# Reordering the first loads and the first matmuls of a gated attention and FFN kernel

## The chip, the cores and the metric

The kernel runs on one core of one Trainium2 chip. The metric is the device time of one execution in microseconds (us). A profile lasts from the first to the last instruction, its span, which is about 1.25 us shorter than the time of the same execution.

## The reference, cut to what matters

```python
x = A_x                                             # 1 x 2048 x 640, bf16
g = sigmoid((x * gate_w).sum(-1, keepdims=True))    # the gate row
a = A_ref(x, A_wqkv, A_w_phi, A_wo)                 # linear attention, 32 heads of 20
b = B_ref(x, B_w_gate, B_w_up, B_w_down)            # (silu(x @ w_gate) * (x @ w_up)) @ w_down
return g * a + (1 - g) * b
```

Three inputs matter here: the rows of x (16 tiles of 128 tokens), the value third of wqkv (five row blocks of 128 x 640, called wv0 to wv4 below), and gate_w (640 numbers, which the kernel transposes and appends to wv as one more column, so that the value product yields the gate's sum as well).

## The kernel before

The program is a list of short codes. `LOADS` gives the order of the transfers, `ORDER` that of the work. H is a pair of dummy matmuls, X a tile's five transposes, G the transpose of the gate row, and U t.c the two products of token tile t with row block c of wv.

```python
NWARM = 2
NPEW = 16
LOADS = """
x0 w0 x1 w1 x2 w2 x3 w3 w4 f0 h k0 k1 t4 ...
"""
ORDER = """
H0 H1 H2 H3 H4 H5 H6 H7 H8 H9 X0 G H10 H11 H12 U0.0 X1 H13 U1.0 U0.1 X2 U1.1 U2.0 U0.2 U1.2 U2.1
X3 U2.2 U0.3 U1.3 U2.3 U0.4 U1.4 U2.4 V3 Y F0.1 M1 ...
"""
# ... (cut)
    XQ = ["sp", "act", "act", "act"]             # queue of x0 to x3
    WQ = ["sp", "sp", "sp", "sp", "act"]         # queue of wv0 to wv4
    dma("act", gwr[0:5, :], bass.AP(gate_w.tensor, gate_w.offset, [[P, 5], [1, P]]))
# ... (cut)
    def xpose(t):                                # X
        pr = next_pair()
        for c0, c1 in (((0, 1), (1, 5)) if t < 3 else ((0, 5),)):
            o = bankbf(2 * pr + (c0 > 0), 640)
            transposes([(o[:, c * P:(c + 1) * P], xs[:, t, c * P:(c + 1) * P]) for c in range(c0, c1)])
            copy("dve", xT[:, t, c0:c1, :].rearrange("p c k -> p (c k)"), o[:, c0 * P:c1 * P])

    def gcol():                                  # G
        pr = next_pair()
        o = bankbf(2 * pr, 8)[:, 0:5]
        transposes([(o, gwr[0:5, :])], 5)
        copy("dve", wvg[:, :, D:D + 1], o.unsqueeze(2))
# ... (cut)
    def kv_end():
        for _ in range(NPEW):
            pe.wait_ge(tr.sem["pe"], 1)          # satisfied long before
        kv_finish()
# ... (cut)
```

The dummy matmuls multiply a constant by itself, and nothing reads what they give.

The softmax here doesn't subtract the row's maximum and nothing guards it: scores larger than these inputs give would overflow.

## Time and profile before

| | before |
|---|---|
| time, three runs | 289.95, 290.13, 290.69 us |
| span of the profiled run | 287.6 us |
| TensorE busy | 284.9 us, 99% |
| TensorE's share of the chain that ended last | 99% |
| first product of the gate projection (`xT,wg`) | 11.49 us after the start |

The lines themselves and their reading stand in the prediction.

```profile
11.49 1.24 PE L296 MATMUL ps<-xT,wg 128*128 128x512 bf16 x5
```

Everything ahead of this line is the start-up that the change touches, and what follows it lasts 287.6 - 11.49 = 276.1 us.

### The profile page before, as it was taken

The numbers are of one execution on the slowest core, as the hardware profiler recorded it, in microseconds if no ns is written. First come the engines' busy times: TensorE is split into PE (matmuls) and PEld (weight loads), VectorE is DVE, ScalarE is ACT, GpSimd is POOL, SyncE is SP. The second block draws the span as 40 slices with busy tenths as digits, with TensorE's granted clock in tenths as the row PEclk, the third lists the DMA queues.
The fourth block names the chain that finished last, engine by engine and source line by source line (L and its number), as shares of the span: only waits on it lengthen the run. The fifth ranks groups of instructions, "written<-read, shape, count | busy, mean of one in ns | idle before, by whom it ended". The sixth has DMA issues, their size and how long they took to land.

```text
span 287.6 us, 4959 instructions
## 1 busy us (share of the span) xinstructions
PE 284.9 (99%) x1977; PEld 175.2 (61%) x1977; DVE 163.4 (57%) x243; ACT 151.8 (53%) x252; POOL 159.8 (56%) x125
## 2 busy tenths in 40 slices
PE   8999999999999999999999999999999999999997
PEld 7667777675644545557775556675554446656776
DVE  2237748576469978689991465970317899100000
ACT  0767778676775565683535653225576552234112
POOL 8286999879446789836543438350753558501000
PEclk9999999999999999999999999999999999999999
DMA  7979488000010598202393002061020006210101
GB/s 219 190 133 123 100 251 317 5 1 2 2 47 0 114 297 162 51 2 50 65 158 70 5 1 50 2 149 42 2 50 0 3 1 123 52 46 0 49 23 48
DMA packets 48944, 21.62 MB, mean 75 GB/s; under 512 B 39384, under 2 KB 48792, under 8 KB 48920
## 3 DMA queue, kind: packets, MB, share of 16 engines
q1 hardware_dynamic: 47534, 20.59, 32.0%
q10 hardware_dynamic: 1386, 0.71, 0.9%
q8 instruction: 16, 0.26, 0.4%
q14 instruction: 8, 0.07, 0.1%
HBM read 9.29 MB, written 2.62 MB: 41 GB/s over the span
## 4 chain that ended last, share of the span: by engine, by line
PE 99%; DVE 0%; issue 0%
PE ps L296 97%; PE ps L477 1%; PE ps L308 1%; DVE osb L732 0%
## 5 line engine op out<-in xcount | busy, mean ns | idle before, releaser
L324 POOL TENSOR_TENSOR hT<-hT,us 128x512 bf16<-128x512 bf16 (+1 forms) x56 | 65.0, 1173 | 65.3 <-DVE hT L328 47.0
L328 DVE SCALAR_TENSOR_TENSOR hT<-hT,ps 128x512 bf16<-128x512 bf16 (+1 forms) x56 | 37.4, 683 | 66.9 <-ACT hT L314 53.3
L296 PE MATMUL ps<-xT,wg 128*128 128x512 bf16 x260 | 64.6, 379 | 0.0
L296 PE MATMUL ps<-xT,wu 128*128 128x512 bf16 x260 | 64.6, 379 | 0.0
L296 PE MATMUL ps<-wd,hT 128*128 128x320 bf16 (+2 forms) x462 | 63.9, 295 | 0.0
L324 POOL TENSOR_TENSOR ph<-eq,qc 128x1320 bf16<-128x1320 bf16 x16 | 42.3, 2644 | 25.6 <-DVE qc L637 22.2
L296 PEld LDWEIGHTS ps<-wd,hT 128*128 128x128 bf16 x462 | 44.5, 98 | 17.4
L296 PE MATMUL ps<-wqk,xT 128*128 128x320 bf16 x320 | 47.7, 299 | 0.0
L314 ACT ACTIVATE hT<-ps 128x512 bf16<-128x512 f32 (+2 forms) x60 | 35.8, 596 | 16.7 <-PE ps L296 16.5
L296 PEld LDWEIGHTS ps<-xT,wu 128*128 128x128 bf16 x260 | 25.5, 98 | 30.6
L314 ACT ACTIVATE us<-ps 128x512 bf16<-128x512 f32 (+1 forms) x56 | 33.5, 598 | 19.2 <-PE ps L296 18.2
L314 ACT ACTIVATE osb<-ps,omg 128x640 bf16<-128x640 f32 (+2 forms) x17 | 12.9, 757 | 55.8 <-PE ps L296 55.8
L296 PEld LDWEIGHTS ps<-xT,wg 128*128 128x128 bf16 x260 | 25.1, 98 | 27.8 <-ACT oT L314 0.8
L324 POOL TENSOR_TENSOR ekr<-ekr,krec 128x1280 bf16<-128x1280 bf16 x16 | 37.4, 2357 | 5.8 <-DVE krec L338 5.8
L296 PEld LDWEIGHTS ps<-wqk,xT 128*128 128x128 bf16 x320 | 30.5, 98 | 13.1 <-issue 0.4
L314 ACT ACTIVATE eq<-ps 128x640 bf16<-128x640 f32 x32 | 22.3, 703 | 20.9 <-POOL ph L324 10.7
L335 DVE TENSOR_REDUCE ksum<-ekr 128x64 f32<-128x1280 bf16 x16 | 23.5, 1470 | 11.7 <-ACT ekr L314 11.7
L314 ACT ACTIVATE ekr<-ps 128x640 bf16<-128x640 f32 x32 | 22.3, 703 | 8.7 <-PE ps L296 8.2
L335 DVE TENSOR_REDUCE qz<-eq 128x64 f32<-128x1280 bf16 x16 | 23.7, 1478 | 2.6 <-ACT eq L314 2.6
L296 PE MATMUL ps<-wog,oT 128*128 128x320 bf16 (+2 forms) x165 | 24.7, 294 | 0.0
L296 PE MATMUL ps<-wvg,xT 128*128 128x320 bf16 (+1 forms) x160 | 24.6, 301 | 0.0
L335 DVE TENSOR_REDUCE qw<-ez 128x64 f32<-128x1280 bf16 x16 | 23.6, 1476 | 0.0
(73 smaller groups left out, 190.4 us busy)
## 6 DMA issues: line engine op xcount, KB each, us to landing
out_dram<-osb SPq DMA_DIRECT2D x15, 160.0 KB, 1.9
wd<-in_B_w_down_dram SPq DMA_DIRECT2D x1, 2080.0 KB, 10.7
wg<-in_B_w_gate_dram SPq DMA_DIRECT2D x1, 1040.0 KB, 10.1
wu<-in_B_w_up_dram SPq DMA_DIRECT2D x1, 1040.0 KB, 12.2
wg<-in_B_w_gate_dram SPq DMA_DIRECT2D x1, 800.0 KB, 6.2
wu<-in_B_w_up_dram SPq DMA_DIRECT2D x1, 800.0 KB, 7.8
wog<-in_A_wo_dram SPq DMA_DIRECT2D x2, 375.0 KB, 7.2
wvg<-in_A_wqkv_dram SPq DMA_DIRECT2D x4, 160.0 KB, 4.2
```

Source lines behind the costliest of these rows:

```text
L296: last = pe.matmul(o, lhsT=l, rhs=r, start=st, stop=sp_, skip_group_check=sk)
L308: last = pe.transpose(o, i, ident[0:k, 0:k])
L314: return run("act", lambda: act.activation(o, i, func, scale=scale), rd, [o])
L324: return run(e, lambda: eo.tensor_tensor(o, a, b, op), [a, b], [o])
L328: return run("dve", lambda: dve.scalar_tensor_tensor(out=o, in0=a, scalar=s, in1=b, op0=op0, op1=op1), rd, [o])
L335: return run("dve", lambda: dve.tensor_reduce(o, i, AX.X, ALU.add), [i], [o])
L477: last = pe.matmul(bank(2 * pr, 0, P), lhsT=c, rhs=c, start=True, stop=True)
```

## The change

The intent, as the diff reads: issue wv0 at once on the queue that nobody else uses yet, fill the wait for x0 with dummies, and bring x1's transposes up so that no dummy stands between the first real products.

```diff
-NPEW = 16
+NPEW = 24
 LOADS = """
-x0 w0 x1 w1 x2 w2 x3 w3 w4 f0 h ...
+x0 w0 x1 g w1 x2 w2 x3 w3 w4 f0 h ...
 ORDER = """
-H0 H1 H2 H3 H4 H5 H6 H7 H8 H9 X0 G H10 H11 H12 U0.0 X1 H13 U1.0 U0.1 X2 ...
+H0 H1 H2 H3 H4 H5 H6 H7 H8 H9 H10 H11 H12 X0 G X1 U0.0 U1.0 U0.1 X2 ...
-    WQ = ["sp", "sp", "sp", "sp", "act"]
+    WQ = ["act", "sp", "sp", "sp", "act"]
-    dma("act", gwr[0:5, :], bass.AP(gate_w.tensor, gate_w.offset, [[P, 5], [1, P]]))
+    def load_gate():
+        dma("sp", gwr[0:5, :], bass.AP(gate_w.tensor, gate_w.offset, [[P, 5], [1, P]]))
```

SyncE's queue now holds x0, gate, wv1, wv2, wv3; ScalarE's holds wv0, x1, x2, x3, wv4. There are 26 dummies instead of 28, all of them in front.

More of the change, by code (lines that the diff above doesn't have):

```diff
@@ L33 @@
 LOADS = """
-x0 w0 x1 w1 x2 w2 x3 w3 w4 f0 h k0 k1 t4 k2 k3 k4 t5 t6 t7 t8 t9 t10 t11 t12 t13 t14 t15 q0 q1 q2 q3
+x0 w0 x1 g w1 x2 w2 x3 w3 w4 f0 h k0 k1 t4 k2 k3 k4 t5 t6 t7 t8 t9 t10 t11 t12 t13 t14 t15 q0 q1 q2 q3
 q4 f1 f2
@@ L38 @@
 ORDER = """
-H0 H1 H2 H3 H4 H5 H6 H7 H8 H9 X0 G H10 H11 H12 U0.0 X1 H13 U1.0 U0.1 X2 U1.1 U2.0 U0.2 U1.2 U2.1
+H0 H1 H2 H3 H4 H5 H6 H7 H8 H9 H10 H11 H12 X0 G X1 U0.0 U1.0 U0.1 X2 U1.1 U2.0 U0.2 U1.2 U2.1
 X3 U2.2 U0.3 U1.3 U2.3 U0.4 U1.4 U2.4 V3 Y F0.1 M1 i3 M0 F0.0 M2 V4 M3 M4 K0 K1 I S0 V6 V5 S1 P0
@@ L752, in _build @@
         "M": lambda m: premult(1, m), "R": lambda m: premult(0, m),
-        "K": ktile, "S": knorm, "P": kmul, "p": lambda t: kmul(t, "dve"), "E": kvtile, "x": load_x, "t": load_xt, "w": load_wv, "h": load_phi, "k": lambda m: load_wt(1, m), "q": lambda m: load_wt(0, m),
+        "K": ktile, "S": knorm, "P": kmul, "p": lambda t: kmul(t, "dve"), "E": kvtile, "x": load_x, "t": load_xt, "w": load_wv, "g": load_gate, "h": load_phi, "k": lambda m: load_wt(1, m), "q": lambda m: load_wt(0, m),
         "f": lambda i: load_ffn(FCUT[i], FCUT[i + 1]), "L": load_late_weights, "T": tail_weights, "J": gates,
```

## The prediction

> **What bounds the kernel now.** I read the page first, then the chain of work that ended last, then the first ten microseconds of the timeline engine by engine, then the DMA view cut to one issue at a time. The page's busy line and the chain:
>
> ```profile
> PE 284.9 (99%) x1977; PEld 175.2 (61%) x1977; DVE 163.4 (57%) x243; ACT 151.8 (53%) x252; POOL 159.8 (56%) x125
> ```
> ```profile
> by line: PE ps L296 97.3%; PE ps L477 1.1%; PE ps L308 0.7%; DVE osb L732 0.1%; issue 0.0%
> ...
> 0.84 2.29 PE ps L477 x20
> 3.14 0.82 PE ps L308 x6
> 3.96 0.75 PE ps L477 x6
> 4.71 0.53 PE ps L296 x2
> 5.24 0.52 PE ps L308 x5
> 5.76 0.11 PE ps L477 x2
> 5.87 0.55 PE ps L296 x4
> ```
>
> TensorE is busy for 99% of the span and the chain never leaves it: L296 are the real matmuls, L308 the transposes, L477 the dummy matmuls that only keep the array busy. No transfer and no other engine is a link. So the program takes as long as its matmul stream, and a change pays only where that stream is not at full rate. The timeline of TensorE shows where that is:
>
> ```profile
> 0.84 2.29 PE L477 MATMUL ps<-const-bfloat16-1.0 128*128 128x128 bf16 x20 [0.84 <-PEq L791]
> 3.13 0.71 PE L308 MATMUL ps<-ident,xs 128*128 128x128 bf16 x5
> 3.77 0.18 PE L308 MATMUL ps<-ident,gwr 5*128 5x5 bf16 x1
> 3.89 0.82 PE L477 MATMUL ps<-const-bfloat16-1.0 128*128 128x128 bf16 x6
> 4.50 0.74 PE L296 MATMUL ps<-wvg,xT 128*128 128x320 bf16 x2
> 5.04 0.72 PE L308 MATMUL ps<-ident,xs 128*128 128x128 bf16 x5
> 5.57 0.30 PE L477 MATMUL ps<-const-bfloat16-1.0 128*128 128x128 bf16 x2
> 5.71 0.71 PE L296 MATMUL ps<-wvg,xT 128*128 128x320 bf16 x4
> 6.26 0.44 PE L308 MATMUL ps<-ident,xs 128*128 128x128 bf16 x5
> ```
>
> Read starts against starts, since the ends are modelled and overlap. Two 128x320 matmuls take 5.04 - 4.50 = 0.54 us, so 0.27 each; four take 6.26 - 5.71 = 0.55, so 0.137 each. Five transposes take 0.53 us at 5.04 and 0.28 at 6.26 (the next start in the trace is 6.54). So the array runs at half speed until about 5.65 us and at full speed from there. From then on successive 128x320 matmuls start 0.135 to 0.141 us apart and 128x512 ones 0.216; the only wider starts in the whole remainder are at the sixty-four-column output items (0.23 to 0.31 us). There is nothing left to gain but in the first 5.7 us, and the whole stake there is small.
>
> [...] 0.27 us then 0.137 us for the same matmul, the change 4.8 us after the first dummy at 0.84. The clock row of the page reads 9 throughout and does not show it. [...] the windows of 0.4 us from 2.2 us on carry 330, 198, 285, 352, 320 and 359 GB/s, whichever of the two queues feeds them. [...]
>
> **The change part by part.**
>
> Dummies: 28 before (20, 6, 2), 26 after, all ahead of the first transposes. Before, the 20 start 0.107 us apart from 0.84. Six more give 20 + 6: first start 0.845, then 0.06 and 24 times 0.107, so the last ends at about 3.57 us instead of 2.93. Before, the array then stood until x0 came: it was issued at 0.80 and landed 2.3 us later, 3.1, and the first transpose is at 3.13. So the six dummies fill a hole of 0.2 us before x0 and push the transposes back to about 3.6. After them the six and the two that stood in the way (4.50 - 3.89 = 0.61 us and 5.71 - 5.57 = 0.14 us) are gone.
>
> Loads: the order before was x0, wv0, wv1, wv2, wv3 on SyncE and gate, x1, x2, x3, wv4 on ScalarE. After: x0, gate, wv1, wv2, wv3 and wv0, x1, x2, x3, wv4. wv0 is issued at 0.82 instead of 1.27 and runs beside x0. Two loads of 160 KB are 328 KB; from about 1.9 us at 320 GB/s that takes 1.0 us, and before, x0's last packet was about 0.5 us ahead of its landing. So x0 should land at 3.4 to 3.6 rather than 3.1, wv0 at 3.4 to 3.6 rather than 3.9. That is just when the 26 dummies end, which is plainly why they were moved. x1 before landed at 1.41 + 2.9 = 4.3. After, it shares with wv1, and three tiles plus part of a fourth must have moved by then, as before: I put it at 4.3 to 4.9, 4.6 in the middle. Later rows come in pairs some 1.2 us apart (x2 landed at 1.80 + 3.9 = 5.7, x3 at 2.27 + 4.8 = 7.1, used at 6.26 and 7.91); these keep slack.
>
> TensorE's order: x0's five transposes (0.53 us at half speed) run 3.6 to 4.15, the gate's one to about 4.25, x1's five start at once if x1 is there, 4.25 to 4.8. Then the first product, which needs VectorE's copies of x0 and of the gate column. Before, that last copy ended at 4.22 + 0.17 = 4.39, which is 0.86 after the last transpose started at 3.53. After, the last transpose starts at about 4.03, so the copy ends at 4.9 and the product runs 4.95 to 5.5, and the second tile's product crosses the speed change and ends at about 5.9. Before, that second product ran 5.71 to 5.98. Gain with everything in time: about 0.1 us. With x1 at 4.6: its transposes run 4.65 to 5.2, the first product to 5.7, the second to 5.97. Gain: 0. With x1 at 4.9: a loss of 0.2 to 0.25 us.
>
> NPEW, 16 waits to 24, each already satisfied when it is met: the waits stand near 75.2 to 76.5 us, where TensorE's sequencer is about 1.5 to 2 us ahead of the array. In that stretch the 20 products of 128x320 start 0.136 apart and the next transposes at 77.58, without a hole. Two waits share one sequencer instruction there, about 0.1 us apart, so eight more take about 0.4 us of a lead of at least 1.0 us. Cost: 0.
>
> Sum: -0.25 to +0.25 us on 290.13, with a centre near -0.1.
>
> **The rivals.** (1) The early load of wv0 delays x0 and x1 on the shared engines and the array waits where the dummies were; x1's transposes now stand ahead of the first product, so a late x1 holds everything behind it. For it: the transfers are at 285 to 359 GB/s there. Against: the total ahead of x1 is the same. It would make 290.3 to 290.6. (2) Fewer holes bring the clock's release earlier[...]: dense dummies from 0.84 to 3.57 instead of stops at 3.1 and 3.7. Against: the stops are only 0.2 and 0.14 us. If it came 1 us earlier, half of the cold microsecond is won, 0.5 us: 289.6. (3) The extra waits starve the array near 76 us: at most 0.4 us, 290.5. (4) All of it is hidden[...]: 290.1 as before, within the runs' own spread of 289.95 to 290.69.
>
> **Range and chances.** The centre is 290.13 - 0.1 = 290.0. The parts differ by at most 0.5 us either way, and the runs of before span 0.7, so 289.4 to 290.7 should hold it 8 times in 10. Two per cent is 5.8 us, more than the entire stretch that the change touches, so same gets nearly all.
>
> **What would show it.** In the new profile: the last dummy at 3.47 and x0's transposes near 3.6; x0's load taking 2.6 to 2.8 us to land instead of 2.3; x1's transposes before 4.7 (gain) or after it (rival 1); the second product's starts at 0.137 spacing from about 5.7 (an earlier change of speed is rival 2); the start of the four later products (6.54 before for the next ones) shifted by under 0.3 us; and no wider starts around 76 to 78 us. The prediction is wrong if a tile that is not here counted lands after TensorE needs it, or if the shift in loads moves a later stage by over a microsecond.

In the trace of before, the two queues' shares of the six stretches of 0.4 us are 329 and 0, 195 and 3, 185 and 99, 70 and 281, 182 and 137, 160 and 198 GB/s (SyncE's first).

## The result, and the profile after

| | before | after |
|---|---|---|
| median time | 289.66 us (6 runs, 289.00 to 290.69) | 288.71 us (6 runs, 288.52 to 289.27) |
| ratio | | 0.9968, interval 0.9946 to 0.9991 |
| span of the profiled run | 287.6 us | 287.3 us |
| first gate product | 11.49 us | 11.14 us |
| from there to the end | 276.1 us | 276.1 us |

A ratio here is the mean time of one kernel's fast runs over that of the other's of the same rounds, so it is not quite the ratio of the medians. In this row the kernel before has six times: the three on record and three new ones (289.38, 289.00, 289.15). All three new ones are below all three old ones, which will matter below.

The busy line of the page after the change, and the chain with its pieces:

```profile
PE 284.5 (99%) x1975; PEld 174.7 (61%) x1975; DVE 163.4 (57%) x243; ACT 151.9 (53%) x252; POOL 159.9 (56%) x125
```
```profile
0.84 2.93 PE ps L478 x26
3.77 1.32 PE ps L308 x11
5.09 0.98 PE ps L296 x6
```

The bound is the same, and the chain is still TensorE from end to end. Its pieces show the new order: 26 dummies in a row, then eleven transposes (x0, gate, x1), then products. The timeline of TensorE after:

```profile
0.84 2.93 PE L478 MATMUL ps<-const-bfloat16-1.0 128*128 128x128 bf16 x26 [0.84 <-PEq L792]
3.76 0.72 PE L308 MATMUL ps<-ident,xs 128*128 128x128 bf16 x5
4.41 0.18 PE L308 MATMUL ps<-ident,gwr 5*128 5x5 bf16 x1
4.53 0.57 PE L308 MATMUL ps<-ident,xs 128*128 128x128 bf16 x5
5.08 0.99 PE L296 MATMUL ps<-wvg,xT 128*128 128x320 bf16 x6
5.92 0.44 PE L308 MATMUL ps<-ident,xs 128*128 128x128 bf16 x5
6.20 1.53 PE L296 MATMUL ps<-wvg,xT 128*128 128x320 bf16 x10
...
11.14 1.24 PE L296 MATMUL ps<-xT,wg 128*128 128x512 bf16 x5
```

Six products take 5.92 - 5.08 = 0.84 us, 0.14 each, so the very first product already runs at full speed. Single transposes change from 0.107 to 0.057 us apart at 4.8 us. I call that moment **the release** of the clock. Before, it came between 5.5 and 5.65 us. x3's transposes start at 7.57 instead of 7.91, and the lead of 0.34 us is carried unchanged to the end.

So this profile shows 0.3 us, while the two medians differ by 0.95. The added waits took nothing: the 20 products around them start at 74.87 and hand over at 77.58 before, and at 74.53 and 77.25 after, 2.71 and 2.72 us. The sequencer's records of the waits stand about 0.11 us apart, up to 75.83 before and 75.91 after. The next wait is recorded at 76.48 and 76.14, 1.10 and 1.11 us ahead of the transpose that follows it.

### The profile page after: what moved, and what is told of

Its sections match the earlier page's. It is cut to its first block, busy times and chain, and to the rows that moved or that the text cites. A ratio compares the mean times of both kernels' runs of the same rounds, so it can differ in the third digit from the quotient of the medians.

```text
span 287.3 us, 4960 instructions
## 1 busy us (share of the span) xinstructions
PE 284.5 (99%) x1975; PEld 174.7 (61%) x1975; DVE 163.4 (57%) x243; ACT 151.9 (53%) x252; POOL 159.9 (56%) x125
## 4 chain that ended last, share of the span: by engine, by line
PE 99%; DVE 0%; issue 0%
PE ps L296 97%; PE ps L478 1%; PE ps L308 1%; DVE osb L733 0%
## 6 DMA issues: line engine op xcount, KB each, us to landing
wu<-in_B_w_up_dram SPq DMA_DIRECT2D x1, 1040.0 KB, 12.8
```

## The experiments

Two theories stood at first. **Clock**: the release falls at another moment in each execution, and the change lets it fall earlier. **Schedule**: the gain is the fixed shift of work that the two profiles show, and the rest is noise. A third, that the **waits** gain something, needed one run. Later a **landing** theory joined them: rows that arrive late hold TensorE in some executions. "Hole" below is the distance between two starts less what the first matmul needs at its speed.

### First call: repeat, and take the change apart

**b_again** is the kernel before, unedited.

> The kernel before, unchanged, for its spread and a second profile. Clock theory: TensorE's change from half to full speed falls at a different moment from execution to execution, the spans spread by more than 1 us, the second profile shows the change later than the first one's 5.65 us, and each us that it comes later lengthens the span by about 0.5 us. Schedule theory: the change comes at 5.65 us again (within 0.2 us), and spans agree within 0.3 us.

Measured: 289.64 us median, 289.02 to 291.51; ratio 1.001 (0.9978 to 1.0041). TensorE's timeline of this second profile of before:

```profile
3.83 0.82 PE L477 MATMUL ps<-const-bfloat16-1.0 128*128 128x128 bf16 x6
4.92 0.70 PE L296 MATMUL ps<-wvg,xT 128*128 128x320 bf16 x2 [0.28 <-DMA wvg<-in_A_wqkv_dram]
5.41 0.74 PE L308 MATMUL ps<-ident,xs 128*128 128x128 bf16 x5
5.94 0.42 PE L477 MATMUL ps<-const-bfloat16-1.0 128*128 128x128 bf16 x2
6.16 1.05 PE L296 MATMUL ps<-wvg,xT 128*128 128x320 bf16 x4
```

Two things differ from the first profile of the same kernel. The four products from 6.16 take 7.04 - 6.16 = 0.88 us instead of 0.55, and single starts change from half to full distance between 6.4 and 6.9: the release came a microsecond later. And TensorE stood before the first product. The six dummies take 0.61 us and end at 4.44, but wv0, issued 1.25 us after the start, landed 3.5 us later at 4.8, where the first profile had it at 3.9. The hole is 0.48 us. The first gate product is at 12.27, and 288.4 - 12.27 is again 276.1. So between these two profiles all of the difference lies in the first 12 us, in two terms that the program does not fix: the moment of the release, and rows that land late.

**loads_only** has the new loads alone.

```diff
-ORDER: H0 ... H12 X0 G X1 U0.0 U1.0 U0.1 X2 ...            NPEW = 24
+ORDER: H0 ... H9 X0 G H10 H11 H12 U0.0 X1 H13 U1.0 ...     NPEW = 16     (against after)
```

> The kernel before with only the new load order; TensorE's order and the 16 waits are those of before. Clock theory: x0's transposes start about 3.75 us instead of 3.13, so the hole after the 20 dummies grows to about 0.8 us; if the clock's release depends on how densely the array was kept busy, it comes late, and the time is 0.3 to 1 us over before. Schedule theory: 0.3 to 0.6 us over before, from x0's later landing alone, with the speed change at 5.65 us.

Measured: 290.74 us median, ratio 1.0034 (1.0009 to 1.0059). Its timeline:

```profile
0.84 2.29 PE L478 MATMUL ps<-const-bfloat16-1.0 128*128 128x128 bf16 x20 [0.84 <-PEq L792]
3.77 0.71 PE L308 MATMUL ps<-ident,xs 128*128 128x128 bf16 x5 [0.63 <-DMA xs<-in_A_x_dram]
...
8.03 2.28 PE L296 MATMUL ps<-wvg,xT 128*128 128x320 bf16 x10
```

x0, with wv0 now issued beside it, lands at 3.72 (in the traces of before and after, which differ alike, ScalarE's queue moved 3 and 166 GB/s from 2.6 to 3.0 us, SyncE's 195 and 192), its transposes start at 3.77, and the 20 dummies are over at 2.93: a hole of 0.84 us. Ten products from 8.03 still take 10.14 - 8.03 = 2.11 us instead of 1.37, so the release came only after 9 us. The loads alone lose 0.8 us in the mean of the timed runs.

**order_only** has the new order alone.

```diff
-ORDER: H0 ... H9 X0 G H10 H11 H12 U0.0 X1 H13 U1.0 ...
+ORDER: H0 ... H12 X0 G X1 U0.0 U1.0 ...                    (against before)
```

> The kernel before with only the new order of TensorE's work (26 dummies first, x1 transposed before the first product); loads and the 16 waits are those of before. Clock theory: the array has no hole until 3.6 us, the release comes near 4.9 us or at least earlier than in before on average, and the time is 0.5 to 1 us under before. Schedule theory: 0.15 to 0.35 us under before, as x0 and x1 are there when they are wanted.

Measured: 289.15 us median, 288.68 to 290.80, ratio 0.9993 (0.9963 to 1.0024). In the mean of the timed runs it is 0.25 us under before, which the schedule theory asked for and the clock theory did not, but the interval of the ratio reaches past 1. In its profile x1 landed at 4.86 and TensorE stood 0.55 us ahead of x1's transposes; the release came at 6.2 us.

**a_npew16** is the changed kernel with 16 waits.

```diff
-NPEW = 24
+NPEW = 16
```

> The changed kernel with the 16 waits of before instead of 24. Clock and schedule theories: the same time as the changed kernel (within 0.2 us; 0.9968 of before). Waits theory (the added waits are what gained): back to the time of before.

Measured: 289.09 us median, ratio 0.9987 (0.9961 to 1.0013). Its interval overlaps that of the result, so by time alone the waits are not settled. Its profile settles it: the first gate product is at 12.95 and the span 289.1, again 276.1 us from there to the end. With 16 or 24 waits the rest of the program is equally long, so the waits theory falls. The late start had another cause:

```profile
6.23 0.71 PE L296 MATMUL ps<-wvg,xT 128*128 128x320 bf16 x4
8.54 1.00 PE L296 MATMUL ps<-wvg,xT 128*128 128x320 bf16 x6 [1.59 <-DMA wvg<-in_A_wqkv_dram]
```

wv2 landed at 8.5 us, and TensorE stood 1.76 us. The changed kernel isn't immune to late rows either.

### Second call: more samples, and the clock on purpose

**a2** and **b2** are the two kernels, unedited.

> The changed kernel, unchanged, for more samples beside the kernel before on one chip. So far every span is the start of the first gate product plus 276.11 us, so all of the spread lies ahead of it. If the first measurement (0.9968) was typical, this repeats 0.995 to 0.998; if a good part of it was luck in where the clock's release fell, it is nearer to the 0.9987 of the version with 16 waits. The second profile shows the speed change somewhere between 3.6 and 7.0 us, and span minus first gate product is again 276.1 us.

> The kernel before, unchanged, a third profile: ratio 1.000 within 0.002; the speed change lies somewhere between 5.6 and 9.6 us; if the late first wv rows of the second profile (4.79 us, a hole of 0.48 us in TensorE) are common, they are seen again.

Measured: a2 288.82 us median (288.68 to 289.23), ratio 0.9987 (0.9973 to 1.0). b2 289.37 (288.46 to 290.16), ratio 0.9996 (0.9979 to 1.0013). a2's profile has its release at 6.0 to 6.5 us and its first gate product at 11.72, so the early release of the first profile after was not a property of the kernel, and the ratio repeats a_npew16's 0.9987 rather than the first 0.9968. b2's profile has the release at 6.5 and a late wv2:

```profile
6.94 0.71 PE L296 MATMUL ps<-wvg,xT 128*128 128x320 bf16 x4
8.38 1.00 PE L296 MATMUL ps<-wvg,xT 128*128 128x320 bf16 x6 [0.73 <-DMA wvg<-in_A_wqkv_dram]
```

That is a hole of 0.90 us (8.38 - 6.94 - 0.55), in the same place as in a_npew16.

**two_dummies** is the changed kernel with one dummy pair.

```diff
-H0 H1 H2 H3 H4 H5 H6 H7 H8 H9 H10 H11 H12 X0 G X1 ...
+H0 X0 G X1 ...
```

> The changed kernel with 2 dummy matmuls instead of 26. Clock theory: [...] the busy time now starts at 3.76 us instead of 0.84, so the speed change comes at 6.4 to 9.8 us, some 2.8 us later, and the time is about 1 to 1.4 us over the changed kernel. Schedule theory: x0 lands at 3.7 us whatever stands before it, so no change (within 0.2 us).

Measured: 289.91 us median, ratio 1.0024 (1.0006 to 1.0041), 1.1 us over a2 by medians. The schedule theory's 0.2 falls. Its timeline:

```profile
3.81 0.71 PE L308 MATMUL ps<-ident,xs 128*128 128x128 bf16 x5 [2.60 <-DMA xs<-in_A_x_dram]
...
5.13 1.79 PE L296 MATMUL ps<-wvg,xT 128*128 128x320 bf16 x6
```

The real work stands about where it stood. Six products take 6.71 - 5.13 = 1.58 us, with the release at 7.0. In the first profile after they took 0.84, but in a2's, of the same call, 6.49 - 4.96 = 1.53, with the release at 6.4: one profile against one shows only 0.37 us of span (288.2 against 287.8). In the mean of the timed runs the dummies are worth 1.2 us. That it comes through the clock is what was expected, and the later release agrees, but the single profile doesn't show the whole of it.

**late_start** is the changed kernel with real work held until the clock and the rows are settled.

```diff
# (shortened)
-H0 ... H12 X0 G X1 ...
+H0 ... H32 X0 G X1 ...
-    memset("pool", ident[:, :], 0.0); select(ident[:, :], ...)      # ahead of GpSimd's fills
+    memset("pool", ident[:, :], 0.0); select(ident[:, :], ...)      # behind fills(0) to fills(2)
```

> The changed kernel with the identity written after GpSimd's other fills (about 8 us, no matter what the clock does) and 66 dummies ahead of x0's transposes, so that real work begins at full speed with all of its rows there. Clock-and-landing theory: about 3.5 us over before, and the spread of the times falls from 2 us to about 0.3 us. If the spread has its source elsewhere, it stays near 2 us.

Measured: 291.70 us median, five runs from 291.69 to 291.79. The shift is 2.5 us rather than 3.5, since GpSimd was done by 7.2 us and not 8. The spread is the point: 0.1 us, where the kernel before had 288.67 to 289.84 in the same call.

```profile
0.84 6.02 PE L479 MATMUL ps<-const-bfloat16-1.0 128*128 128x128 bf16 x66 [0.84 <-PEq L793]
7.21 0.44 PE L308 MATMUL ps<-ident,xs 128*128 128x128 bf16 x5 [0.35 <-POOL ident L356]
```

Five transposes from 7.21 hand over to the gate's at 7.58, at full speed. With the release over and all but x3, wv3 and wv4 landed when real work starts, the spread goes. So it comes from the start-up, from the release and the landings together; this run does not part the two.

### Third call: late rows, and the hole filled

**a3**, **b3** (both unedited) and **order_only2** (order_only again):

> The changed kernel again, for samples and a third profile. Landing theory: wv0 lands by 4.0 us once more (3.77 to 3.97 in all six profiles with it at the head of ScalarE's queue so far), no hole over 0.3 us before the first product, ratio 0.996 to 0.999. Clock theory: the speed change anywhere from 3.6 to 7.0 us.

> The kernel before again, for samples and a fourth profile. Landing theory: wv0 lands anywhere between 3.9 and 4.8 us; where it is over 4.4, a hole stands before the first product. Ratio 1.000 within 0.002.

> TensorE's new order with the loads of before, again, for a second profile: wv0 behind x0 on SyncE lands after 4.4 us, beside x1, and TensorE stands 0.2 us or more ahead of the first product; ratio 0.997 to 1.001. If wv0 lands by 4.0 us here too, its place in the queue is not what matters.

Measured: a3 288.87 us, ratio 0.9992 (0.9974 to 1.0009), just above the 0.996 to 0.999 expected. b3 289.13, ratio 1.0005 (0.9984 to 1.0026). order_only2 289.03, ratio 0.9993 (0.9977 to 1.0009). a3's wv0 landed at 3.9 as expected, but wv2 was late by 0.36 us. b3's wv0 landed at 4.1 without a hole, and its wv1 was late by 0.90 us. order_only2 missed its expectation: wv0 landed at 4.0 and x1 at 4.2, with no hole. The old queue order does not make those two rows late, it only lets them be late in some executions.

order_only2 and the next run, fill_hole, show another place where a late transfer can hold TensorE: from the first gate product to the end they last 276.28 and 276.27 us, not 276.12. w_phi landed at 12.2 and 12.8 us in them, and the first products that use what VectorE and GpSimd make of it start 0.17 and 0.15 us late.

**fill_hole** is loads_only with four more dummy pairs ahead of x0.

```diff
-H0 ... H9 X0 G H10 H11 H12 U0.0 X1 H13 U1.0 ...
+H0 ... H9 H14 H15 H16 H17 X0 G H10 H11 H12 U0.0 X1 H13 U1.0 ...
```

> The new load order with TensorE's order of before, but four more dummy pairs ahead of x0's transposes, so that the 0.84 us hole of the loads-only version is filled and the last dummy ends as x0 lands. Clock theory [...]: most of the 1.2 us mean loss of the loads-only version comes back, 0.2 to 0.5 us over before on average, and no speed change after 7.2 us. Row theory (the loss was x0's later landing alone, x0's transposes still start at 3.77): the same 290.6 us as the loads-only version.

Measured: 289.72 us median (289.44 to 290.18), ratio 1.0022 (1.0006 to 1.0038). The release came at 6.1 us, so the expectation of no speed change after 7.2 held. Against the kernel before of its own call it is 0.6 us slower in the mean of the timed runs, just over the 0.2 to 0.5 expected, and loads_only 0.8 us in its own. The times alone don't decide, since the two intervals overlap and each call ran on another chip. The profiles say more: x0's transposes start at 3.78 and 3.77 in the two, and the first gate product at 12.13 and 13.72. The row theory, which wants these equal, falls for this pair.

### Fourth call: an attempt to take the clock out, which failed

All loads and all real work wait for GpSimd's fills, behind 72 more dummies, in the four combinations of old and new loads with old and new order.

```diff
+    for _ in range(36):
+        warm()
+    for e in ("sp", "act", "pe"):
+        tr._wait(e, {"pool": tr.cnt["pool"]})
     for w in LOADS.split() + ORDER.split():
```

(In the two with the old loads, the gate's transfer was moved behind the wait too.)

> The kernel before with all of its loads and its real work held until GpSimd's fills are done (about 7.2 us), behind 72 more dummies: the array is at full speed when x0 lands. About 5 us over before. Both theories: the spread left is that of the landings alone; under the clock theory most of the 0.6 us standard deviation is gone (0.2 us or less), under the rows theory it stays at 0.4 us or more.

> The same for the changed kernel. Rows theory (a): it keeps 0.3 us or more of its lead over the kernel before treated alike. Clock theory (b): the lead is under 0.15 us or is lost, since at full speed x0's later landing (3.7 against 3.1 us after the same start) is no longer hidden by dummies.

> The same for the new loads with TensorE's old order. In the plain kernels it lost 0.8 to 0.9 us, with the speed change at 9.4 us. Clock theory: most of that loss came from the release put off by the 0.84 us hole, so here it loses at most 0.4 us to the kernel before treated alike. Row theory: it loses 0.6 us or more here too.

> The same for TensorE's new order with the old loads. Row theory: as the kernel before treated alike or up to 0.3 us under it, and 0.1 us or more over the changed kernel treated alike. Clock theory: within 0.15 us of the kernel before treated alike.

Measured medians: s_before 297.29 us, s_after 298.07, s_loads 298.32, s_order 296.98, ratios to the kernel before 1.0276, 1.0302, 1.0322 and 1.0256, with spreads of 1.5 to 1.9 us. No spread shrank. The windows view shows why; here it is for s_order, with its columns length, TensorE busy (matmuls), granted clock, DMA share and GB/s:

```profile
9.00:11.10 2.10, 0.10 (x2) 1.00 0.98 293
12.95:16.25 3.30, 3.30 (x18) 0.50 1.50 288
16.50:19.00 2.50, 2.50 (x23) 1.00 0.90 150
```

The loads, issued at 7.2 us, took 3.9 us to bring x0, where the same load issued at 0.8 takes 2.3. TensorE stood idle from about 9.0 to 11.17 us. The granted clock read 1.00 over that stretch, 0.50 from 12.95 to 16.25 us, and 1.00 again from 16.50. Real work that should have run at full speed ran at half: the ten products from 13.78 take 16.39 - 13.78 = 2.61 us instead of 1.37. The four runs tell nothing about what they were made for. They do show a granted clock of 0.50 after an idle stretch: here after 2.1 us, and in s_before, from 12.3 to 15.6 us, after 2.6 us.

### Fifth call: the last pair

> The changed kernel once more: 0.3 to 0.4 us under the kernel before in the mean of the timed runs, largest time under 289.6 us; in the profile wv0 by 4.0 us, and span minus first gate product 276.1 us. If the gain of the earlier calls was chance, the mean lies within 0.1 us of before.

> The kernel before once more: mean of the timed runs 289.1 to 289.8 us with times over 290 among them; in the profile wv0 at 3.9 to 4.8 us, and at the same moment of the clock's release and without holes for late rows its first gate product within 0.1 us of the changed kernel's plus 0.07.

Measured: a4 289.01 us, ratio 0.9991 (0.9977 to 1.0004), and 0.24 us under before in the mean of the timed runs, a little less than expected. b4 289.30, ratio 1.0000 (0.9987 to 1.0013); no time over 290 us this time. a4's profile has the release at 5.2 and holes of 0.26 us for wv1; b4's has the release at 6.3 to 6.7 and none.

### What the ten profiles say together

All times in us. "Holes" are those ahead of late rows, and the last column is the first gate product less these holes. In b_again the hole stood ahead of the release: it displaced work from half speed to full speed, so only about half of it is lost and its last column is too low by some 0.24 us (an estimate from 0.27 and 0.137 us a product before and after the release).

| profile | release | wv0 landed | holes | first gate product | less holes |
|---|---|---|---|---|---|
| before | 5.5 to 5.65 | 3.9 | 0 | 11.49 | 11.49 |
| b_again | 6.4 to 6.9 | 4.8 | 0.48 | 12.27 | 11.79 |
| b2 | 6.5 | 4.4 | 0.90 | 12.79 | 11.89 |
| b3 | 5.3 | 4.1 | 0.90 | 12.34 | 11.44 |
| b4 | 6.3 to 6.7 | 4.0 | 0 | 11.93 | 11.93 |
| after | 4.8 | 3.9 | 0 | 11.14 | 11.14 |
| a_npew16 | 4.1 to 4.6 | 4.0 | 1.76 | 12.95 | 11.19 |
| a2 | 6.0 to 6.5 | 3.8 | 0 | 11.72 | 11.72 |
| a3 | 6.3 | 3.9 | 0.36 | 12.12 | 11.76 |
| a4 | 5.2 | 3.9 | 0.26 | 11.47 | 11.21 |

Compare at one release. b3 and a4, at 5.3 and 5.2: 11.44 and 11.21; b2 and a3, at 6.5 and 6.3: 11.89 and 11.76. From b3 to b2 a release one microsecond later costs about (11.89 - 11.44) / 1.14 = 0.4 us. Brought to the same release the changed kernel leads by about 0.19 us in the first pair and by 0.05 to 0.08 in the second. That is the part of the change that the schedule fixes: 0.05 to 0.2 us, from two pairs.

A record that was not used above confirms these moments. Most of the packed traces keep when the granted clock changed. (The windows view can't show the release: it reads 1.00 before the first of these records too.) The releases read from the starts agree with it: 5.61 in before, 6.46 in b2, 5.32 in b3, 4.81 in after, 6.34 in a3, 5.22 in a4.

What sets the moment is not shown. The program alone does not: the release lies anywhere from 5.3 to 6.9 us in the five profiles of the kernel before, and from 4.1 to 6.5 in those of the changed kernel. loads_only and fill_hole make a pair in which more of TensorE's time was filled: from 2.7 to 6.1 us, counted from the starts, it was busy for about 68% in the first, with the hole of 0.84 us, and the release came at about 9.55; with the hole filled it was busy for about 92%, and the release came at 6.11. That is one profile of each. The earlier releases of the changed kernel's profiles may be luck.

The timed runs, without the profiled executions, give per call (mean of the changed kernel less mean of the kernel before, the latter's new runs alone): -0.32 at the result, -0.37 with a2, -0.30 with a3, -0.24 with a4; a_npew16, whose waits change nothing, has -0.65 in the first call and is not counted below. Each call ran on another chip. Over all calls the kernel before has 75 such runs, mean 289.32, median 289.20, range 288.46 to 291.51. The changed kernel has 19, mean 288.89, median 288.88, range 288.53 to 289.28. The gain is 0.3 us, 0.1%.

**What stays open**: where the 0.1 to 0.25 us beyond the schedule's part come from. In these profiles the holes are alike (2.28 and 2.38 us in five profiles of each kernel). The releases of the changed kernel are earlier by some 0.7 us in the mean, which at 0.4 us each would be 0.3 us; but each kernel's releases spread over 1.5 to 2 us, and five of each can't tell such a difference from chance. wv0 itself did land more evenly with its new place: 3.8 to 4.0 in five profiles against 3.9 to 4.8. No tested version beat the changed kernel beyond the noise: the new order with the old loads has the same mean gain, 0.25 and 0.30 us, with single times up to 290.8.

## Why the prediction was right or wrong

- **The bound: right for the steady part.** TensorE is 99% busy before and after, and all ten profiles of the two kernels have 276.1 us after the start-up. "No transfer and no other engine is a link" holds for the profile that it was read from, but in six of the ten a late row held TensorE, for 0.26 to 1.76 us.
- **The added waits: right.** They cost nothing, and gained nothing.
- **The landings: partly off, in both directions.** x0 came at 3.7 us, not 3.4 to 3.6 (2.9 us from issue instead of the 2.6 to 2.8 expected). x1 came at 4.26, not 4.6, and so was there when its transposes were due at 4.5; the predicted wait for it did not come in any profile with the new loads. The rival "late x1" falls. The rows that did come late, wv1 and wv2 (a4, a3, a_npew16, and b3 and b2 without the change), are in no rival; the prediction's own sign of being wrong, a tile not counted that lands after TensorE needs it, came true for them.
- **The path through VectorE: right.** Its last copy was to end 0.86 us after x0's last transpose starts. It ended at 4.86 + 0.17 = 5.03, after a start at 4.17, and the first product followed at 5.08; 4.95 was predicted, from an earlier x0.
- **The sum of the schedule, "about 0.1 us with everything in time": right in size.** At one release the runs show 0.05 to 0.2.
- **The rival of an earlier release** was put aside with "the stops are only 0.2 and 0.14 us". In the first profile after, the release did come 0.8 us earlier; but with a2, a3 and a4 it lies anywhere from 4.8 to 6.5. That the change causes it is not shown.
- **The fourth rival**, that all of it is hidden, was right in kind but too narrow: it put the runs' own spread at 289.95 to 290.69.
- **The step that failed is the anchor of the range**: "the centre is 290.13 - 0.1 = 290.0 ... and the runs of before span 0.7, so 289.4 to 290.7". It took three runs as the kernel's time and their width as its width. Of 75 later runs seven are above 290 and the median is 289.20; the three are all above 289.9. The profile that the prediction read was itself a shorter execution than any of them: its own time is 288.91 us, which fits its span of 287.6, so the anchor could have been doubted beforehand. Whether the three were chance or something of that occasion no run tells. This accounts for 0.9 of the 1.3 us between 290.0 and 288.71. The gain, 0.3 instead of 0.1, accounts for 0.2, and the last 0.2 is that the six runs of the result lie below the changed kernel's own 288.88.
- **The headline 0.9968 flatters the change** for the same reason: against the three new runs of before alone, the five timed runs give 288.86 / 289.18 = 0.9989, as in the later calls.

## What to carry to other kernels

Subtract before you explain: if the span less the first steady instruction is the same number in every profile, all of the spread and all of the change lie in the start-up, and one profile is one draw of it. Hold the profiled execution's own time against the timed runs before you anchor on either. A gain smaller than the kernel's own spread can't be forecast from three runs, nor confirmed by six; put the range around the spread, not around the median. Here TensorE bounds and starts at half speed, and a gap of 0.84 us in front of the first real work went with a loss of more than its own length: loads_only's first gate product came 1.6 us after fill_hole's, though x0's transposes start at the same time, and its release 3.4 us later. So try to fill such a gap with dummies up to the moment the first rows land. That more dummies would only delay the work is reasoning; no run here tried it.
